# Softmax sums inverted in one narrow tile by way of DRAM, and a third key tile added on VectorE

## The chip, the cores and the metric

The kernel runs on one NeuronCore of a Trainium2 chip. The metric is device time in microseconds (us) of one execution; the kernel before took 1294.06 us (median of three runs).

## The reference

All data are float32. An attention block with normalised queries and keys is followed by a two-layer feed-forward block:

```python
# q, k, v: (8 batches, 12 heads, 448 positions, 64)
q_n, k_n = rmsnorm(q, g_q), rmsnorm(k, g_k)
scores = q_n @ k_n.T / sqrt(64)
attn = exp(scores - max)
attn = attn / (sum(attn) + 1e-9)
x = (attn @ v)           # heads side by side: 3584 tokens x 768
h = x @ w_in             # 768 x 2048
out = (h * sigmoid(h)) @ w_out   # 2048 x 768
```

## The kernel before, in words

**Couples.** The attention is done in 24 couples, numbered c = 0 to 23. A couple is four heads of one batch, and six couples (`GROUP`) make two batches. Each head has three tiles of 128 keys, `weights(c, 0)` to `weights(c, 2)`, and 64 keys left over, `left_weights(c)`. All exponentials lie in SBUF with the keys on the partitions and the 448 queries on the columns. Products with V (`weigh`) accumulate in two PSUM banks, `av0` and `av1`.

**The sums.** The softmax needs the sum of the exponentials over the keys, that is, over partitions. VectorE first adds key tile 1 into key tile 0 (`add(c, 1)`, L803). Then TensorE multiplies with a tile of ones (`sum_up`, L832): one term is four matmuls, 128 rows by 32 columns of ones, by 448 columns. For couples 0 to 4 there are three terms: key tile 2, the added tile 0, and the left-over keys. The result `t`, in a PSUM bank, holds four heads' sums, each repeated on 32 partitions.

**The inverses.** VectorE inverts `t` in two halves of 224 columns (`invert`, L841) into `sums_x`, and `spread` copies the inverses between partitions with six SBUF-to-SBUF transfers of 56 KB on the SP queue (L854 four times, and L856 twice, which wait for the former). `factors(c)` are two tiles of 128x448 in `sums_x`, taken in turn by even and odd couples. `divide(c)` (L863) multiplies the attention output of couple c with them. For couples 0 to 4 it runs late: `divide(c - 2)` stands in the visit of couple c, and `divide(3)` and `divide(4)` stand in the program after couple 4 and after couple 5. Before that VectorE has copied `av0` and `av1` out of PSUM (L1514), which frees the two banks for the next couple's `weigh`. From couple 6 on VectorE divides straight out of PSUM.

**Order.** Everything in the attention is issued by hand, engine by engine; an engine runs its instructions in the program's order and so does the SP queue, on which nearly all transfers are issued. `visit(c)` holds the scores, exponentials and products with V, `between(c)` the transposes for the next couple, the sums, and pieces of other work: `room.w_in.round()` rounds W (L126, L129, L133 on VectorE, then L137 on POOL) and loads further pieces of it (L88), and from couple 3 on TensorE is given feed-forward products (L963). Lists of closures carry work from one place to the next: for couples 0 to 2 the two closures that `sum_up` yields wait in `inverting`, of which the first runs in the middle of the next visit and the second at its end; for couples 3 and 4 they run in `between(c)`.

The order in visit(c + 1) of VectorE's work that touches this: the norm's first sum (L475), the two copies out of PSUM (L1514), the first half of the inverse, `divide`, two more norm sums, `add`, the second half of the inverse, the rounding of W.

Of the kernel before, what the change touches and what calls it, by code (L numbers as in the profile page):

```python
# [11 lines left out]
F32 = mybir.dt.float32  # L12
# [18 lines left out]
class Shapes:  # L31
    def __init__(self, q, w_in):
# [8 lines left out]
        self.HALF = self.DM // 2  # L41
        self.FULL = self.S // self.P
        self.REST = self.S - self.FULL * self.P

# [498 lines left out]
def bounded(  # L543
# [3 lines left out]
    P, D, R, J, S = z.P, z.D, z.R, z.J, z.S  # L547
    HW, HF = z.NW // 2, z.NF // 2
    mem = ctx.enter_context(tc.tile_pool(name="mem", bufs=1))
    dram = ctx.enter_context(tc.tile_pool(name="dram", bufs=1, space=bass.MemoryType.DRAM))  # L550
# [6 lines left out]
    GROUP, LATE = z.NPAIR, z.LATE  # L557
    EARLY = GROUP - 1
    SOON = 2 * GROUP - 1
    FULL = (GROUP, SOON - 1)  # L560
    LAGGED = [c for c in range(SOON - 1, NC) if c % GROUP != GROUP - 1]


    hidden = dram.tile([z.NF, P, z.B * S], F32, name="hidden")


    sets = [mem.tile([P, 2 * z.NW * S], F32, name=f"x{i}") for i in range(2)]
    sums_x = mem.tile([P, 3 * HW * S], F32, name="sums_x")
    stage = mem.tile([P, 3 * 2 * S], F32, name="stage")
    parts = mem.tile([P, 2 * S], F32, name="parts")  # L570
    work = mem.tile([P, 16 * S + z.NK], F32, name="work")
    at = 0

# [7 lines left out]
    e = [piece(4 * S).rearrange("p (i h s) -> p i h s", i=2, h=2) for _ in range(3)]  # L581
# [11 lines left out]
    n = 2 * room.COLS  # L593
# [29 lines left out]
    def factors(c):  # L623

        if c >= EARLY:
            return r
        return [sums_x[:, ts(c % 2 * 2 + i, S)] for i in range(2)]
# [9 lines left out]
    LEFT = z.KEYS  # L637
# [56 lines left out]
    n = z.NK // z.Q  # L694
# [99 lines left out]
    def add(c, j):  # L794

        def one(i):
            total = weights(c, 0)[:, i]
            if j == LEFT:
                rows = ds(i * D, D)
                total, more = total[rows], left_weights(c)[rows]  # L800
            else:
                more = weights(c, j)[:, i]
            nc.vector.tensor_tensor(out=total, in0=total, in1=more, op=ALU.add)  # L803

        return [lambda: one(0), lambda: one(1)]

    def sum_up(c):

        n = D // 2
        early = c < GROUP
        if c < GROUP:
            t = bank(S)
        elif c in LAGGED:
            t = ps_mm.tile([P, BANK], F32, name="mm")[:, 0:S]
        else:
            t = ps.tile([P, 2, BANK], F32, name="sc", bufs=2)[:, 0, 0:S]
        terms = [(0, lambda: weights(c, 0))]  # L820
        if early:
            terms = [(0, lambda: weights(c, LEFT - 1))] + terms + [(1, None)]
        if c in FULL:
            terms.insert(0, (1, None))
        if c == GROUP - 1:
            terms.insert(1, (0, lambda: weights(c, 1)))
        for k, (which, w) in enumerate(terms):
            if early and k == len(terms) - 2:
                yield
            for h in range(2):  # L830
                for i in range(2):
                    nc.tensor.matmul(  # L832
                        t[ds(h * D + i * n, n), :],
                        ones[:, which + i if which else 0],
                        left_weights(c)[:, h] if which else w()[:, i, h],
                        start=(k == 0), stop=(k == len(terms) - 1),
                    )

        def invert(half):
            rows = ts(half, S // 2)  # L840
            nc.vector.reciprocal(out=factors(c)[0][:, rows], in_=t[:, rows])  # L841

        def spread():
            mine = [a.rearrange("(h i p) s -> i h p s", h=2, i=2) for a in factors(c)]
            queues = (nc.sync, nc.gpsimd if c == GROUP - 1 else nc.sync)
            if c >= EARLY:
                nc.vector.tensor_copy(factors(c)[1], factors(c)[0])
                for i in range(2):
                    for h in range(2):
                        queues[h].dma_start(mine[i][1 - i, h], mine[i][i, h])  # L850
                return
            for h in range(2):
                for i in range(2):
                    nc.sync.dma_start(mine[1][i, h], mine[0][1, h])  # L854
            for h in range(2):
                nc.sync.dma_start(mine[0][1, h], mine[0][0, h])  # L856

        yield [lambda: invert(0), lambda: (invert(1), spread())]

    def divide(c, source):  # L860
        for i in range(2):
            x = x_of(c, i)
            nc.vector.tensor_tensor(  # L863
                out=x, in0=x if source is None else source[i], in1=factors(c)[i], op=ALU.mult
            )
# [618 lines left out]
    def visit(c):  # L1484

        beside = normalise(c + 1) if 0 < c <= GROUP else []
        if c == GROUP:
            beside = [lambda: None] + beside[2:]
        if c < NC:
            scores(c, 0, 0)  # L1490
        for step in visits.get(c, "")[:1]:
            step_of[step]()
        if lagging:
            lagging.pop(0)()
        if c == 0:
            first_q(1)
            normalise_alone(1)
            scores(c, 1, 0)
        if c == 0:
            run_all(beside[0:1])  # L1500
        else:
            weigh(c - 1, LEFT)
            weigh(c - 1, LEFT - 1, 0)
            turn(1, nc.scalar.copy if c <= GROUP else nc.vector.tensor_copy)
            run_all(beside[0:1])
            if GROUP < c < NC and c % GROUP == 0:
                sum_x(last_two(c), 0, range(2, 4))
        if c < NC:
            scores(c, 0, 1)
        if c > 0:  # L1510
            weigh(c - 1, LEFT - 1, 1)
            if c - 1 < EARLY:
                for i in range(2):
                    nc.vector.tensor_copy(x_of(c - 1, i), sums[i])  # L1514
                run_all(beside[1:2])
                if c == GROUP // 2 + 1:
                    divide(c - 2, None)
                if inverting:
                    while len(inverting) > 1:
                        inverting.pop(0)()  # L1520
                    if c > 1:
                        divide(c - 2, None)
            else:
                if lagging:
                    for i in range(2):
                        nc.vector.tensor_copy(x_of(c - 1, i), sums[i])
                    lagging.pop(0)()
                else:
                    divide(c - 1, sums)
                if c == GROUP:  # L1530
                    for i in range(1, HW):
                        sum_x(last_two(c), i, range(2))
                    for i in range(2):
                        norm.scale(c + 1, q_of(c + 1), q_of(c + 1), i, nc.vector)
                    room.w_in.round()
                run_all(beside[1:2])
                if GROUP < c < NC and c % GROUP == 0:
                    for i in range(1, HW):
                        sum_x(last_two(c), i)
                weights_in_visit(c)  # L1540
            if c + 1 < NC:
                loads["vrest"](c + 1)
        if c == NC:
            return
        if c > 0:
            scores(c, 1, 0)
        scores(c, 1, 1)
        if c <= GROUP:
            run_all(beside[2:3])
        weigh(c, 0, 1)  # L1550
        scores(c, 2, 0)
        weigh(c, 1, 1)
        turn(0, nc.scalar.copy)
        if c < GROUP:
            run_all(beside[3:4])
        scores(c, 2, 1)
        weigh(c, 0, 0)
        if c < GROUP:
            scores(c, LEFT)
        if c != GROUP - 1:  # L1560
            run_all(add(c, 1))
        weigh(c, 1, 0)
        if c < GROUP // 2:
            room.w_in.open()
        if c >= GROUP:
            scores(c, LEFT)
        if c + 1 < NC:
            loads["v"](c + 1)
        if len(inverting) == 1:
            inverting.pop()()  # L1570

    def run_all(work):
        for piece in work:
            piece()

    def between(c):
# [47 lines left out]
        late = add(c, LEFT - 1) if c >= GROUP else []  # L1624
        if c >= GROUP and c not in FULL:
            late += add(c, LEFT)
# [48 lines left out]
            while rounder.load():  # L1675
                pass

    begun, inverting, lagging = {}, [], []
    load_q(2)
    for _ in range(2):  # L1680
        room.w_in.load()
# [23 lines left out]
    for m in range(2):  # L1705
        rows = [staged() for _ in range(2)]
# [8 lines left out]
def general(  # L1715
# [130 lines left out]
    def feed_forward(b):  # L1846
        odd = b % 2
        own = mp.tile([P, z.NF, z.FULL * P], F32, name="g_own")
        if not odd:
# [72 lines left out]
```

## Time and profile before

| what | value |
|---|---|
| time of three runs | 1293.84, 1294.06, 1294.23 us |
| profiled execution, first to last instruction | 1294.6 us (0.5 us over the median of the runs) |
| TensorE busy | 1283.5 us, 99% of the span |
| VectorE busy | 971.4 us, 75% |
| ScalarE busy | 504.3 us, 39% |
| GpSimd busy | 363.5 us, 28% |
| granted TensorE clock, mean | 0.999 |
| couples 0 to 4, on TensorE | from 9 to 94 us |

The share of a busy engine is a mean over stages. The part that the change touches is the first tenth of the span, where couples 0 to 5 run with little or no feed-forward work between them, so it is read in windows of that stretch. Rows of a timeline give the start, the length, the engine, the line and the tiles of a run of like instructions, and behind that the idle time of the engine before it with what ended it. A float32 matmul stands in the records twice, so four matmuls of the program read as x8.

### The profile page before, as it was taken

To read this page: it belongs to the slowest core of one execution; us is meant where nothing else is said; L and a number is where in the kernel's file an instruction comes from. 1 tells how busy PE (TensorE), PEld (TensorE's weight loads), DVE (VectorE), ACT (ScalarE), POOL (GpSimd) and SP (SyncE) were. 2 spreads that over 40 slices of the span, in tenths; PEclk is the share of its full clock that TensorE was granted. 3 is DMA by queue.
4 is the path that set the end of the run, shared out by engine and by line. 5 is a ranking of instruction groups with operands and counts; after the bars stand their busy time and mean duration, and the time that the engine had idled before them with its cause. 6 is when DMAs were issued, how large, how long until landed. Compare 5 with 4: busy or idle time off the path is not lost.

```text
span 1294.6 us, 19931 instructions
## 1 busy us (share of the span) xinstructions
PE 1283.5 (99%) x7212; PEld 840.7 (65%) x7212; DVE 971.4 (75%) x1672; ACT 504.3 (39%) x880; POOL 363.5 (28%) x221
## 2 busy tenths in 40 slices
PE   9999999999999999999999999999999999999998
PEld 4444454444444454444544555559999999999998
DVE  6898878868666558666555886798978787878785
ACT  7967666645555554554543344310001000000000
POOL 6765454543344344343311344400000000000000
PEclk9999999999999999999999999999999999999999
DMA  9675347434444444444411466312332313141411
GB/s 232 174 193 136 104 124 197 95 83 102 112 94 91 119 91 102 108 93 93 107 50 69 149 204 219 117 66 88 100 94 86 113 67 129 51 133 48 141 39 40
DMA packets 266160, 144.15 MB, mean 111 GB/s; under 512 B 203748, under 2 KB 249956, under 8 KB 266052
## 3 DMA queue, kind: packets, MB, share of 16 engines
q1 hardware_dynamic: 265424, 141.68, 39.8%
q8 instruction: 59, 0.97, 0.3%
q0 software_dynamic: 320, 0.90, 0.2%
q14 instruction: 49, 0.40, 0.1%
q10 hardware_dynamic: 308, 0.20, 0.1%
HBM read 95.36 MB, written 41.29 MB: 106 GB/s over the span
## 4 chain that ended last, share of the span: by engine, by line
PE 97%; DVE 1%; POOL 1%; issue 0%; ACT 0%; DMA 0%; SPq 0%; ACTq 0%; DVEq 0%; POOLq 0%
PE alone L1285 23%; PE mm L963 21%; PE sc L963 11%; PE av L789 10%; PE sc L752 10%; PE mm L1285 8%; PE alone L963 7%; PE alone L1323 2%; PE mm L832 2%; PE mm L1323 1%; PE sc L643 1%; PE sc L832 1%; PE sc L674 0%; DVE work L912 0%; POOL rms L503 0%
## 5 line engine op out<-in xcount | busy, mean ns | idle before, releaser
L757 ACT ACTIVATE work<-sc,rms 128x448 f32<-128x448 f32 x318 | 182.0, 635 | 98.0 <-PE sc L752 85.7
L752 PE MATMUL sc<-work 64*64 64x448 f32 x1344 | 169.4, 543 | 1.0 <-ACT work L653 0.6
L789 PE MATMUL av<-work,rows 64*64 64x448 f32 x1272 | 155.5, 540 | 1.2 <-DVE x L1514 0.9
L963 PE MATMUL mm<-x,W 128*128 128x448 f32 x366 | 149.1, 542 | 0.0
L963 PE MATMUL mm<-sums_x,W 128*128 128x448 f32 x348 | 142.4, 542 | 0.0
L803 DVE TENSOR_TENSOR work<-work 128x896 f32<-128x896 f32 (+1 forms) x110 | 118.3, 1105 | 28.6 <-PE av L789 28.1
L530 POOL DMA_DIRECT2D out_dram<-x x2 | 1.2, 592 | 443.5 <-DVE x L912 443.5
L503 POOL TENSOR_TENSOR rms<-rms,minus_half 128x14 f32<-128x14 f32 (+4 forms) x40 | 97.4, 2437 | 86.8 <-DVE rms L499 83.3
L963 PEld LDWEIGHTS mm<-x,W 128*128 128x128 f32 x366 | 68.5, 190 | 70.3 <-issue 64.8
L1285 PE MATMUL alone<-W,rows 128*128 128x192 f32 x610 | 113.0, 326 | 0.0
L963 PEld LDWEIGHTS mm<-sums_x,W 128*128 128x128 f32 x348 | 65.1, 190 | 68.1 <-issue 62.5
L789 PEld LDWEIGHTS av<-work,rows 64*64 64x64 f32 x1272 | 65.9, 132 | 62.8 <-issue 19.3
L752 PEld LDWEIGHTS sc<-work 64*64 64x64 f32 x1344 | 60.4, 132 | 63.3 <-ACT work L757 25.3
L1285 PEld LDWEIGHTS alone<-W,rows 128*128 128x128 f32 x610 | 101.4, 190 | 0.0
L963 PE MATMUL sc<-x,W 128*128 128x448 f32 x246 | 99.6, 541 | 0.0
L984 POOL TENSOR_TENSOR stage<-parts,stage 128x448 f32<-128x448 f32 x31 | 39.8, 1285 | 169.2 <-ACT stage L983 168.9
L722 POOL TENSOR_TENSOR rms<-rms,minus_half 128x28 f32<-128x28 f32 x15 | 72.6, 4842 | 48.9 <-DVE rms L719 47.8
L963 PEld LDWEIGHTS sc<-x,W 128*128 128x128 f32 x246 | 46.4, 190 | 47.0 <-issue 46.7
L1285 PE MATMUL alone<-W,work 128*128 128x192 f32 x382 | 72.2, 326 | 0.0
L1295 ACT COPY rows<-alone 128x192 f32<-128x192 f32 x33 | 10.5, 318 | 141.5 <-PE alone L1285 136.7
L1285 PEld LDWEIGHTS alone<-W,work 128*128 128x128 f32 x382 | 63.8, 190 | 0.0
L1116 ACT ACTIVATE stage<-stage 128x896 f32<-128x896 f32 x63 | 56.8, 945 | 17.1 <-DVE stage L912 16.9
(267 smaller groups left out, 2312.8 us busy)
## 6 DMA issues: line engine op xcount, KB each, us to landing
hidden<-stage SPq DMA_DIRECT2D x63, 448.0 KB, 2.9
work<-hidden SPq DMA_DIRECT2D x21, 1024.0 KB, 5.1
rows<-in_moe_w_out_dram SPq DMA_DIRECT2D x32, 384.0 KB, 3.7
W<-in_moe_w_in_dram SPq DMA_DIRECT2D x22, 512.0 KB, 5.3
x<-hidden SPq DMA_DIRECT2D x7, 1024.0 KB, 6.1
rows<-in_q_dram SPq DMA_DIRECT2D x120, 56.0 KB, 2.2
rows<-in_k_dram SPq DMA_DIRECT2D x120, 56.0 KB, 2.3
rows<-in_k_dram SPq DMA_DIRECT2D x60, 96.0 KB, 2.6
```

The costliest lines, as they stand in the source:

```text
L503: nc.gpsimd.tensor_tensor(out=t, in0=t, in1=half, op=ALU.pow)
L722: nc.gpsimd.tensor_tensor(out=f, in0=f, in1=minus_half.to_broadcast([P, n]), op=ALU.pow)
L752: nc.tensor.matmul(two[ds(half * D, D), h, 0:S], keys[rows, ts(half, D)], qT[rows, pair, :], start=True, stop=True,)
L757: nc.scalar.activation(left_weights(c)[:, h] if j == LEFT else weights(c, j)[:, i, h], two[:, h, 0:S], AF.Exp, scale=norm.column(c, i, h, j),)
L789: nc.tensor.matmul(sums[i][ds(h * D, D), :], v, w, start=(j == 0 and step == 1), stop=(j == LEFT - 1 and step == 1),)
L803: nc.vector.tensor_tensor(out=total, in0=total, in1=more, op=ALU.add)
L832: nc.tensor.matmul(t[ds(h * D + i * n, n), :], ones[:, which + i if which else 0], left_weights(c)[:, h] if which else w()[:, i, h], start ...
L963: nc.tensor.matmul(t, self.left(name, s), self.right(name, s), start=s == ends[0], stop=s == ends[1])
L984: nc.gpsimd.tensor_tensor(out=done[1, 2], in0=u2, in1=p5, op=ALU.add)
L1116: nc.scalar.activation(t, t, AF.Silu)
L1285: nc.tensor.matmul(t, x[:, i], y, start=i == ORDER[0], stop=i == ORDER[-1])
L1323: nc.tensor.matmul(o, a[:, 2 * i + m, t], right_one(name, i)[:, m], start=n == 0, stop=n == len(steps) - 1,)
```

## The change

For couples 0 to 4 the inverses take another way. `gather` copies `t` from PSUM to SBUF, and a transfer lays one row for each head (four rows of 448) out as 128 partitions by 14 columns in a new tile `spot`. `invert_all` inverts `spot`, stores it in a DRAM tile `totals` (four rows of 448, one such tile for even and one for odd couples), and a last transfer reads it back into `sums_x`: the first two rows side by side (896 numbers) on partitions 0 to 63, the last two on 64 to 127. For couples 0 to 2 the two closures stand where the halves of the inverse stood; for couples 3 and 4 `gather` stands in `between(c)` and `invert_all` in the visit of the next couple. From couple 5 on nothing changes.

For couples 0 to 2 VectorE also adds key tile 2 into tile 0, and the product with ones has two terms, first the left-over keys, then the added tile.

```diff
+    LIGHT = GROUP // 2
+    totals = [dram.tile([4, S], F32, name=f"totals{i}") for i in range(2)]
+    spot = mem.tile([P, 4 * S // P], F32, name="spot")
...
         terms = [(0, lambda: weights(c, 0))]
-        if early:
+        if c < LIGHT:
+            terms = [(1, None)] + terms
+        elif early:
             terms = [(0, lambda: weights(c, LEFT - 1))] + terms + [(1, None)]
...
-            if early and k == len(terms) - 2:
+            if early and k == max(1, len(terms) - 2):
                 yield
...
-            for h in range(2):
-                for i in range(2):
-                    nc.sync.dma_start(mine[1][i, h], mine[0][1, h])
-            for h in range(2):
-                nc.sync.dma_start(mine[0][1, h], mine[0][0, h])
-        yield [lambda: invert(0), lambda: (invert(1), spread())]
+        def gather():
+            t_sums = factors(c)[0]
+            nc.vector.tensor_copy(t_sums, t)
+            rows = t_sums.rearrange("(n p) s -> n p s", n=4)[:, 0]
+            nc.sync.dma_start(spot, rows.rearrange("n (p e) -> n p e", p=P // 4))
+        def invert_all():
+            d = totals[c % 2]
+            nc.vector.reciprocal(out=spot, in_=spot)
+            nc.sync.dma_start(d.rearrange("n (p e) -> (n p) e", p=P // 4), spot)
+            source = d.rearrange("(h one i) s -> h one (i s)", one=1, i=2)
+            nc.sync.dma_start(sums_x[:, ts(c % 2, 2 * S)], source.to_broadcast([2, D, 2 * S]))
+        if c < LIGHT:
+            yield [gather, invert_all]
+        elif c < EARLY:
+            spreading.append(invert_all)
+            yield [gather]
+        else:
+            yield [lambda: invert(0), lambda: (invert(1), spread())]
...  visit(c)
+                if spreading:
+                    spreading.pop()()
...
+        if c < LIGHT:
+            run_all(add(c, LEFT - 1))
```

In the kernel with the change the lines stand a little further down: L803 is L806, L832 is L837, L863 is L880, and the new lines are L858 and L860 (`gather`) and L864, L865 and L867 (`invert_all`).

VectorE in the visit of couple 2 and behind it, where couple 0 is divided and couple 1 inverted, before (`x` is the attention output or, in L475, the squares; `mm` is the bank of the sums):

```order
L841 RECIPROCAL sums_x<-mm 128x224
L863 TENSOR_TENSOR x_172<-x_172,sums_x 128x448 x2
L475 TENSOR_REDUCE rms_61<-rows 128x8
L475 TENSOR_REDUCE rms_61<-x_173 128x6
L499 TENSOR_SCALAR rms_61<-rms_61 128x14
L803 TENSOR_TENSOR work<-work 128x896 x2
L841 RECIPROCAL sums_x<-mm 128x224
L126 TENSOR_SCALAR W<-W 128x512
```

and now:

```order
L858 COPY sums_x<-mm 128x448
L880 TENSOR_TENSOR x_174<-x_174,sums_x 128x448 x2
L475 TENSOR_REDUCE rms_61<-rows 128x8
L475 TENSOR_REDUCE rms_61<-x_175 128x6
L499 TENSOR_SCALAR rms_61<-rms_61 128x14
L806 TENSOR_TENSOR work<-work 128x896 x4
L864 RECIPROCAL spot<-spot 128x14
L126 TENSOR_SCALAR W<-W 128x512
```

Each half of the inverse has become one short instruction, the adds are four instead of two, and the order around them is as it was.

The SP queue from the visit of couple 1 on, where couple 0's sums are handled (`rows` are inputs of q, k and v), before:

```order
L273 DMA x_173<-in_q_dram 112x4x256
L331 DMA rows<-in_v_dram 128x4x64
L334 DMA rows<-in_v_dram 64x2x64 x2
L318 DMA rows<-in_v_dram 128x4x128
L854 DMA sums_x<-sums_x 32x448 x4
L856 DMA sums_x<-sums_x 32x448 x2
L294 DMA rows<-in_k_dram 128x6x64
```

and now:

```order
L273 DMA x_175<-in_q_dram 112x4x256
L860 DMA spot<-sums_x 128x1x14
L331 DMA rows<-in_v_dram 128x4x64
L334 DMA rows<-in_v_dram 64x2x64 x2
L318 DMA rows<-in_v_dram 128x4x128
L865 DMA totals_172<-spot 128x14
L867 DMA sums_x<-totals_172 128x1x896
L294 DMA rows<-in_k_dram 128x6x64
```

The six short copies are gone, a transfer of 7 KB has come in ahead of the loads of V, and a store of 7 KB and a read of 448 KB ahead of those of K.

More of the change, by code (lines that the diff above doesn't have):

```diff
@@ L845, in spread @@
             queues = (nc.sync, nc.gpsimd if c == GROUP - 1 else nc.sync)
-            if c >= EARLY:
-                nc.vector.tensor_copy(factors(c)[1], factors(c)[0])
-                for i in range(2):
-                    for h in range(2):
-                        queues[h].dma_start(mine[i][1 - i, h], mine[i][i, h])
-                return
-            for h in range(2):
-                for i in range(2):
-                    nc.sync.dma_start(mine[1][i, h], mine[0][1, h])
-            for h in range(2):
-                nc.sync.dma_start(mine[0][1, h], mine[0][0, h])
-        yield [lambda: invert(0), lambda: (invert(1), spread())]
+            nc.vector.tensor_copy(factors(c)[1], factors(c)[0])
+            for i in range(2):
+                for h in range(2):
+                    queues[h].dma_start(mine[i][1 - i, h], mine[i][i, h])
+        def gather():
[16 more added lines that the diff above has]
+            yield [lambda: invert(0), lambda: (invert(1), spread())]
     def divide(c, source):
@@ L1676, in between @@
                 pass
-    begun, inverting, lagging = {}, [], []
+    begun, inverting, spreading, lagging = {}, [], [], []
     load_q(2)
```

## The prediction

> **What bounds the kernel now.** I read the page's busy shares and its chain of waits first, then windows of the stretch where the change sits, then the timeline of VectorE at the divisions, since these consume what the change makes.
>
> ```profile
> PE 1283.5 (99%) x7212; PEld 840.7 (65%) x7212; DVE 971.4 (75%) x1672; ACT 504.3 (39%) x880; POOL 363.5 (28%) x221
> PE 97%; DVE 1%; POOL 1%; issue 0%; ACT 0%; DMA 0%; SPq 0%; ACTq 0%; DVEq 0%; POOLq 0%
> ```
>
> TensorE works 1283.5 of 1294.6 us and the chain runs along it. Little can be won but TensorE's own work; much can be lost if it is made to wait. The next rows are windows: length, then busy time of PE, PEld, DVE, ACT and POOL, the granted clock, the DMA share and GB/s.
>
> ```profile
> 30.00:60.00 30.00, 29.91 (x298) 12.59 (x294) 25.95 (x39) 27.27 (x52) 21.99 (x14) 1.00 0.75 206
> 60.00:90.00 30.00, 28.58 (x242) 13.13 (x246) 27.62 (x38) 22.76 (x43) 21.79 (x13) 1.00 0.63 165
> 104.94:116.91 11.97, 11.97 (x109) 5.31 (x105) 11.62 (x17) 8.38 (x15) 6.91 (x6) 1.00 0.30 73
> ```
>
> In this stretch VectorE, 75% busy over the span, is at 87%, 92% and 97%. It runs in order, so what stops it there is made up slowly. These are its five divisions by the factors in question, `divide(0)` to `divide(4)`, then the first direct division of couple 6 and TensorE's weight load behind it:
>
> ```profile
> 46.57 1.09 DVE L863 TENSOR_TENSOR x<-x,sums_x 128x448 f32<-128x448 f32 x2
> 63.31 1.97 DVE L863 TENSOR_TENSOR x<-x,sums_x 128x448 f32<-128x448 f32 x2 [1.28 <-DMA sums_x<-sums_x]
> 80.37 2.01 DVE L863 TENSOR_TENSOR x<-x,sums_x 128x448 f32<-128x448 f32 x2
> 91.27 1.15 DVE L863 TENSOR_TENSOR x<-x,sums_x 128x448 f32<-128x448 f32 x2
> 104.94 1.81 DVE L863 TENSOR_TENSOR x<-x,sums_x 128x448 f32<-128x448 f32 x2 [0.19 <-DMA sums_x<-sums_x]
> 116.91 1.16 DVE L863 TENSOR_TENSOR x<-av,work 128x448 f32<-128x448 f32 x2
> ```
>
> ```profile
> 117.89 0.52 PEld L789 LDWEIGHTS av<-work,rows 64*64 64x64 f32 x8 [0.23 <-issue]
> ```
>
> Two of the five already wait for the last copy of the spread. The row at 116.91 reads `av` out of PSUM, and TensorE's next product into `av` starts at 117.89 behind it: there, late factors become late TensorE.
>
> **The change part by part.** Prices, by groups of the first 135 us (busy time, mean ns of one):
>
> ```profile
> L841 DVE RECIPROCAL sums_x<-mm 128x224 f32<-128x224 f32 x10 | 15.3, 1543 | 0.0
> L1514 DVE COPY x<-av 128x448 f32<-128x448 f32 x10 | 5.7, 617 | 0.0
> L499 DVE TENSOR_SCALAR rms<-rms 128x14 f32<-128x14 f32 x7 | 1.7, 238 | 0.2
> L803 DVE TENSOR_TENSOR work<-work 128x896 f32<-128x896 f32 x10 | 11.3, 1173 | 0.0
> ```
>
> *VectorE.* Per couple, two inverses (3.09 us) go; a copy of 128x448 (0.62, by L1514) and an inverse of 128x14 come. The latter has no row: it lies between a 128x14 operation of another kind (0.24) and the old inverse (1.54); cost per column is what the inverse's rows show (1.54 for 224), and I take 0.2. VectorE gains 2.3 us in each of five couples. Two more adds cost couples 0 to 2 about 2.1 us each (row at 33.65, below). So its work shrinks by 11.4 - 6.3 = 5 us; its order is kept, so its waits decide.
>
> *TensorE.* One term of the sums goes from couples 0 to 2:
>
> ```profile
> 36.66 0.96 PE L832 MATMUL mm<-work,ones 128*32 128x448 f32 x8
> 37.44 0.94 PE L832 MATMUL mm<-x,ones 128*32 128x448 f32 x8
> 38.19 0.94 PE L832 MATMUL mm<-work,ones 128*32 128x448 f32 x8
> 33.65 2.10 DVE L803 TENSOR_TENSOR x<-x,work 128x896 f32<-128x896 f32 x2
> ```
>
> From start to start a term takes 0.76, so 2.3 us in all. But the added tile now needs four adds: they start at 33.65 and end at 37.8 (2.05 later than before), while its term would start at 37.44, so about 0.4 is waited in each couple. Net -1.1, between -2.3 (adds early) and 0.
>
> *The transfers.* Six copies of 56 KB become three steps, each waiting for the one before: spot, the 7 KB store, and the 448 KB read.
>
> ```profile
> 33.58 0.33 SPq L273 DMA_DIRECT2D x<-in_q_dram  x1
> 40.67 2.80 SPq L856 DMA_DIRECT2D sums_x<-sums_x  x2
> x<-in_q_dram SPq DMA_DIRECT2D x1, 448.0 KB, 5.1
> DMA to landing us min/median/max: 1.9/2.7/7.8
> ```
>
> Spot is queued right behind a q load, which for couple 0 takes 5.1 us from 33.9; so spot lands at 38.9, 1.1 after the adds end. VectorE, which formerly had its data in PSUM, now waits for a transfer ahead of each inverse; behind it are queued the rounding of W, the next norm sums and the copies out of `av`, and on SP, behind the store and the read that wait for the inverse, the K and W loads. The store, at 7 KB, gets the smallest landing of the tile's copies, 1.9, and 0.2 to start: 2.1.
>
> The read has no counterpart. It takes two source rows, each 64 times: 128 pieces of 3584 bytes. Its price hangs on how many DMA engines carry it. Nearest from the side of large ones, a plain 448 KB transfer between DRAM and SBUF, whose two sides have 128 rows:
>
> ```profile
> stage<-ahead SPq DMA_DIRECT2D x1, 448.0 KB, 3.6
> ```
>
> And from the side of few rows, the two loads of the gains, one row each; they alone are on queue 10 of the first 115 us. Last come the packets while the two L856 copies, 32 rows each, run, and a saturated window.
>
> ```profile
> q10 hardware_dynamic: 4, 0.00, 0.0%
> W<-in_g_q_dram ACTq DMA_DIRECT2D x1, 0.2 KB
> W<-in_g_k_dram ACTq DMA_DIRECT2D x1, 0.2 KB
> DMA packets 75, 0.09 MB, mean 35 GB/s; under 512 B 32, under 2 KB 74, under 8 KB 74
> 32.00:34.00 2.00, 2.00 (x21) 0.67 (x20) 1.10 (x4) 2.00 (x5) 1.65 (x3) 1.00 1.04 408
> ```
>
> Each copy left 16 packets under 512 bytes: one end mark for each engine. The gain loads left four packets in two transfers, so one of data and one mark each: one engine. The count of engines thus follows the rows that a transfer steps through. 408 GB/s at a share of 1.04 is 24.5 GB/s an engine. 458,752 bytes then take 1.2 us on 16, 9.4 on two, 18.7 on one; with 1.9 to land, 3.1, 11.3 and 20.6. The ends are 3.1 and 20.6. I take two engines, 11.3, since the outermost step of the source counts two rows and the nearest case, a count of one, got one engine.
>
> [...]
>
> *The sum.* Couple 0: spot 38.9, inverse 0.2, store 2.1, read 11.3: 52.5, where `divide(0)` stood at 46.57. VectorE stands there, and the next inverse is behind it: one turn of a loop. The norm sums between take 1.4 by these starts:
>
> ```profile
> 47.58 0.68 DVE L475 TENSOR_REDUCE rms<-rows 128x8 f32<-128x512 f32 x1
> 48.96 2.10 DVE L803 TENSOR_TENSOR work<-work 128x896 f32<-128x896 f32 x2
> ```
>
> Couple 1: division 1.1, norm sums 1.5, four adds 4.1, about 1 for spot (two of its engines are still draining), then 13.6 (0.2, 2.1, 11.3): 73.8 against 63.31. Couple 2, two adds fewer and spot in time: 1.1 + 1.5 + 2.1 + 13.6 = 18.3, so 92.1 against 80.37. Couple 3's inverse stands right behind `divide(2)`, without adds, but its spot stands behind loads on the two engines: about 1.9 MB are under way, a sixteenth of it each, an estimated 5.4 with landing; with 13.6 that is 19.0: 111.1 against 91.27. Couple 4 likewise, 19.5 with the longer division row: 130.6 against 104.94. The factors are 25.7 late. From there VectorE is busy 11.62 of 11.97 us, so 0.3 is regained up to 116.91, and TensorE at 117.89 starts its product 25.4 late. TensorE's net gain of 1.1 lies ahead of that wait and is swallowed. TensorE then is the bound again and cannot make it up. Against the profiled execution 1294.6 + 25.5 = 1320.1; that execution stands 0.5 over the median of the runs, so 1319.6, rounded to 1320. This case's own range is 1306 (half of each wait hidden) to 1338 (the K loads, queued behind the read, add 3 us to each turn).
>
> **The rivals.** *First: 16 engines carry the read, no change.* It lands in 3.1 to 3.6, and only spot makes VectorE late.
>
> ```profile
> 60.36 0.98 PE L789 MATMUL av<-x,rows 64*64 64x448 f32 x8 [0.45 <-DVE rms L475]
> 79.19 1.13 PE L789 MATMUL av<-work,rows 64*64 64x448 f32 x6 [0.94 <-DVE x L1514]
> 74.89 2.96 DVE L841 RECIPROCAL sums_x<-mm 128x224 f32<-128x224 f32 x2
> ```
>
> The wait at 60.36 grows by some 1.5 through VectorE's spot waits; the one at 79.19 (0.94) goes, as the pair of inverses ahead of that copy out of PSUM becomes a 0.62 copy; `divide(4)`, which already waits, gets 1 later; the products bring -1.1. 1294.1 + 1.5 - 0.9 + 1.0 - 1.1 = 1294.6, about 1295. For it: all large transfers here run on 16, and the destination does have 128 partitions. Against it: the one-row loads.
>
> *Second, not slower: faster, by hidden transfers.* If spot lands before the adds end (37.8 for couple 0) and the read in under 4 us, VectorE never waits. Then the products bring -1.1, the wait at 79.19 -0.94, that at 60.36 -0.45, and that of 104.94 -0.19: 1291.4. Against it: the q load's 5.1 us, which holds spot until 38.9.
>
> *Third: the read runs on some number between.* On four engines it takes 4.7 + 1.9 = 6.6, each turn is 4.7 shorter, and the five turns leave few microseconds: 1298 to 1306. Nothing in the trace speaks for it but that two ends are known.
>
> **How the numbers follow.** Two engines 0.74, the first rival 0.18, the second 0.04, the third 0.04. About 0.2%, 2.6 us, is what a measurement of this kernel can tell from no change. The forecast and the third rival are slower; of the first, 0.14 is within 2.6 us, 0.02 each beyond. That gives faster 0.06, same 0.14, slower 0.80. The range 1292 to 1338 takes in most of the first rival and leaves out the second and the forecast's upper tail.
>
> **What the changed profile would show.** Right: the reads from `totals` land some 11 us after issue, and the DMA busy share is low while they run; VectorE's divisions wait for DMA with `sums_x<-totals`, and start near 52, 74, 92, 111 and 130; TensorE has idle stretches adding up to some 25 us between 50 and 145, ended by copies or divisions on VectorE; behind that, all rows are those of before, shifted. The term of the sums behind four adds shows a wait of about 0.4. Wrong: reads that land in under 4 us (the first two rivals); an inverse of 128x14 near 1 us; or a granted clock under 1.00 behind the long idle stretches, which would put time on top that the sum lacks.

## The result and the profile after

The changed kernel takes 1327.91 us (median of five runs, 1324.57 to 1330.07) against 1294.10: a ratio of 1.0255, 95% interval 1.0244 to 1.0265, slower by 33.8 us. The forecast was 1320, range 1292 to 1338.

First the page of the changed kernel, then its windows (columns as before).

```profile
PE 1293.8 (98%) x7188; PEld 846.5 (64%) x7188; DVE 965.5 (73%) x1678; ACT 504.1 (38%) x880; POOL 360.8 (27%) x221
PE 92%; DMA 4%; DVE 2%; ACT 1%; SPq 0%; issue 0%; ACTq 0%; DVEq 0%
sums_x<-totals SPq DMA_DIRECT2D x5, 448.0 KB
```

```profile
30.00:60.00 30.00, 25.96 (x230) 11.04 (x226) 21.01 (x35) 23.04 (x43) 18.43 (x12) 0.94 0.67 202
60.00:90.00 30.00, 27.28 (x231) 11.07 (x229) 19.36 (x35) 19.81 (x39) 16.97 (x11) 0.95 0.35 102
129.50:144.85 15.35, 10.57 (x89) 4.62 (x81) 10.82 (x18) 6.79 (x13) 3.14 (x3) 1.00 0.21 56
```

DMA has come into the chain of waits, with 4%. TensorE does fewer matmuls and is nevertheless busy 10 us longer, and the granted clock, 1.00 in all three windows before, is 0.94 and 0.95 in the first two. VectorE, 87%, 92% and 97% busy in the three windows before, is now at 70%, 65% and 70%: it stands idle more of the time. Its timeline tells where: these are the five late divisions, now L880, and the first direct one.

```profile
51.57 1.16 DVE L880 TENSOR_TENSOR x<-x,sums_x 128x448 f32<-128x448 f32 x2 [5.41 <-DMA sums_x<-totals]
74.39 1.16 DVE L880 TENSOR_TENSOR x<-x,sums_x 128x448 f32<-128x448 f32 x2 [6.30 <-DMA sums_x<-totals]
93.52 1.16 DVE L880 TENSOR_TENSOR x<-x,sums_x 128x448 f32<-128x448 f32 x2 [4.31 <-DMA sums_x<-totals]
112.87 1.16 DVE L880 TENSOR_TENSOR x<-x,sums_x 128x448 f32<-128x448 f32 x2 [6.05 <-DMA sums_x<-totals]
133.86 1.16 DVE L880 TENSOR_TENSOR x<-x,sums_x 128x448 f32<-128x448 f32 x2 [8.13 <-DMA sums_x<-totals]
144.85 1.16 DVE L880 TENSOR_TENSOR x<-av,work 128x448 f32<-128x448 f32 x2
```

All five wait for the read, 30.2 us together. The reads themselves stand in the DMA rows. The issue of couple 0's read comes first, then the DMA share (in tenths) and the rate from 40.3 to 52 us, in 40 slices of 0.29 us.

```profile
40.31 0.56 SPq L867 DMA_DIRECT2D sums_x<-totals  x1
```

```profile
DMA  0000100399611111111311431114215795311965
GB/s 0 0 0 0 25 25 37 104 236 275 177 53 49 49 49 49 49 61 49 105 49 49 110 86 74 49 54 121 70 58 144 184 227 151 109 59 32 191 106 160
```

Between 43.8 and 45.9 us the rate is 49 GB/s in six slices of seven, at a share of 0.12 (two of 16): two engines at 24.5 GB/s and fourteen empty. The trace has the read as 128 packets of 3584 bytes, 0.144 us each in the median, and they run from 41.64 to 51.06, two at a time on average. From the issue at 40.31 to the division at 51.57 are 11.3 us; for the others, by their issues (62.91, 81.91, 101.33, 122.67), 11.2 to 11.6.

TensorE's waits in the stretch from 50 to 146 us that are over 1 us, all behind VectorE, none behind a DMA:

```profile
57.06 2.72 PE L837 MATMUL mm<-work,ones 128*32 128x448 f32 x8 [4.04 <-DVE work L806]
77.86 1.59 PE L837 MATMUL mm<-x,ones 128*32 128x448 f32 x5 [2.64 <-DVE x L806]
102.10 1.59 PE L837 MATMUL mm<-work,ones 128*32 128x448 f32 x5 [3.00 <-DVE work L806]
118.97 2.29 PE L792 MATMUL av<-x,rows 64*64 64x448 f32 x8 [5.62 <-DVE x L1531]
145.53 2.29 PE L792 MATMUL av<-work,rows 64*64 64x448 f32 x8 [5.46 <-DVE x L880]
```

The last is the product into `av` that the prediction puts at 117.89. That is the row of its weight load, which is 27.6 us later now. The matmuls themselves stood here before:

```profile
118.26 0.93 PE L789 MATMUL av<-work,rows 64*64 64x448 f32 x8
```

They are 27.3 us later. Over the next 5 us of work the distance grows, and from the matmuls that stood at 123 us before on to the last one, all stand 30.0 to 30.3 us later than in the first profile.

### The profile page after: what moved, and what is told of

It is laid out like the page before. It is cut to its first block, busy times and chain, and to the rows that moved or that the text cites. A ratio compares the mean times of both kernels' runs of the same rounds, so it can differ in the third digit from the quotient of the medians.

```text
span 1324.7 us, 19869 instructions
## 1 busy us (share of the span) xinstructions
PE 1293.8 (98%) x7188; PEld 846.5 (64%) x7188; DVE 965.5 (73%) x1678; ACT 504.1 (38%) x880; POOL 360.8 (27%) x221
## 4 chain that ended last, share of the span: by engine, by line
PE 92%; DMA 4%; DVE 2%; ACT 1%; SPq 0%; issue 0%; ACTq 0%; DVEq 0%
PE alone L1302 22%; PE mm L980 20%; PE sc L980 11%; PE av L792 9%; PE sc L755 9%; PE mm L1302 8%; PE alone L980 7%; DMA sums_x<-totals 3%; PE alone L1340 2%; PE mm L837 1%; DMA spot<-sums_x 1%; PE mm L1340 1%; PE sc L837 1%; DMA totals<-spot 0%; DVE work L929 0%; DVE x L880 0%
## 5 line engine op out<-in xcount | busy, mean ns | idle before, releaser
L755 PE MATMUL sc<-work 64*64 64x448 f32 x1344 | 175.6, 554 | 1.0 <-ACT work L656 0.7
L792 PE MATMUL av<-work,rows 64*64 64x448 f32 x1272 | 160.3, 549 | 5.7 <-DVE x L880 5.5
L806 DVE TENSOR_TENSOR work<-work 128x896 f32<-128x896 f32 (+1 forms) x114 | 121.5, 1096 | 28.9 <-PE av L792 28.4
L755 PEld LDWEIGHTS sc<-work 64*64 64x64 f32 x1344 | 63.9, 135 | 63.4 <-ACT work L760 24.2
L980 PEld LDWEIGHTS sc<-x,W 128*128 128x128 f32 x246 | 46.4, 190 | 47.1 <-issue 46.5
```

The costliest lines, as they stand in the source:

```text
L755: nc.tensor.matmul(two[ds(half * D, D), h, 0:S], keys[rows, ts(half, D)], qT[rows, pair, :], start=True, stop=True,)
L792: nc.tensor.matmul(sums[i][ds(h * D, D), :], v, w, start=(j == 0 and step == 1), stop=(j == LEFT - 1 and step == 1),)
L980: nc.tensor.matmul(t, self.left(name, s), self.right(name, s), start=s == ends[0], stop=s == ends[1])
```

## The experiments

**The kernel before, once more.**

> The kernel before, unchanged, profiled once more. The profiled execution shown for it took 1296.4 us, 2 us over the median of its runs. Expected: a span near 1292.5 us; where its rows stand earlier than those of the profile shown tells which 2 us of that profile were its own. All theories expect the same here.

It took 1294.29 us, with a span of 1292.5. From 14 to 57 us its matmuls agree with those of the first profile within 0.06 us, and from 80 us on they stand 1.9 us earlier on average. So the waits of 0.45 and 0.94 us at 60.36 and 79.19 of that first profile, on which two rivals of the prediction counted, belonged to that execution: here no wait of TensorE behind VectorE is listed between 14 and 170 us.

**The read in two.** Instead of one read with two source rows, one for each half:

```diff
-            nc.sync.dma_start(sums_x[:, ts(c % 2, 2 * S)], source.to_broadcast([2, D, 2 * S]))
+            for h in range(2):
+                out = sums_x[ds(h * D, D), ts(c % 2, 2 * S)]
+                nc.sync.dma_start(out, source[h].to_broadcast([D, 2 * S]))
```

> The changed kernel, with the 448 KB read issued as two reads of 224 KB, one for each half of the partitions; each now steps through 64 rows on both sides (the one stored row, 64 times with stride zero, into 64 partitions). Nothing else differs. Theory A (the read is slow because its outermost step counts two, so that two DMA engines carry it): each read runs on 16 engines, lands within 3 to 4.5 us of its issue, the DMA rate while it runs is far above the 49 GB/s of the changed kernel, the five divisions start within 2 us of those of the kernel before (46.6, 63.3, 80.4, 91.3, 104.9), and the time is 1293 to 1298 us; I take 1295. Rival B (the three-step chain is the culprit: spot behind the q load, the inverse on VectorE behind spot, the store, whatever carries the read): the read lands sooner, but at least a third of the loss stays, 1305 us or more. Rival C (repeating one DRAM row 64 times is itself slow, at any number of engines): reads still land 8 us or more after issue, 1315 us or more.

It took 1299.03 us, ratio 1.0032 (1.0021 to 1.0044): 28.9 of the 33.8 us are gone. The rows are a window from the middle of couple 0's reads, the median landing of the ten, and couple 4's division:

```profile
42.30:45.50 3.20, 2.69 (x30) 0.75 (x24) 3.17 (x6) 3.20 (x7) 2.43 (x2) 1.00 0.98 219
sums_x<-totals SPq DMA_DIRECT2D x10, 224.0 KB, 4.0
108.69 1.16 DVE L882 TENSOR_TENSOR x<-x,sums_x 128x448 f32<-128x448 f32 x2 [4.07 <-DMA sums_x<-totals]
```

The DMA share is 0.98 instead of 0.12. Rivals B and C fall. But 4.6 us over the kernel before stay, four over theory A's figure and one over its range: `divide(4)` still waits 4.07 us, since its store and read together take 8 us behind the inverse. TensorE waits 2.06 us behind that division and 1.4 us, in two waits, behind copies out of PSUM.

**62 and 2 rows instead of 64.** The same two reads, each cut once more:

```diff
+                for first, n in ((0, 62), (62, 2)):
+                    out = sums_x[ds(h * D + first, n), ts(c % 2, 2 * S)]
+                    nc.sync.dma_start(out, source[h].to_broadcast([n, 2 * S]))
```

> As the run with two reads (64 partitions each), but each of the two is cut into one of 62 partitions and one of 2: the same source row, the same bytes, the same targets, two issues more. Theory A (the number of engines follows the number of rows stepped through; 62 has no divisor up to 16 but 2 and 1): two engines carry all of it, 49 GB/s while they run, reads land 10 us or more after issue, and the loss is back: 1315 to 1335 us. Rival (what was slow was one transfer with a source of two rows, or the broadcast as a single transfer): 1297 to 1302 us, as with 64.

It took 1332.88 us, ratio 1.0297 (1.0279 to 1.0314): the whole loss is back, and 5 us more. These are the DMA rows from 43 to 50 us and couple 0's division:

```profile
DMA  2214345589930111110211262111144111136899
GB/s 76 85 60 114 94 116 117 145 198 218 240 98 29 61 61 41 41 41 20 82 41 41 76 173 78 42 61 61 47 133 123 66 41 61 41 105 184 219 278 266
52.14 1.16 DVE L883 TENSOR_TENSOR x<-x,sums_x 128x448 f32<-128x448 f32 x2 [6.26 <-DMA sums_x<-totals]
```

Bytes, source and targets are those of the run before; 64 has become 62 and 2, with two more issues for each couple. Between these two runs it is the number of rows that decides (a DMA share of 0.98 with 64 above, digits of 0 to 2 from 45.1 to 46.8 us here), neither the broadcast nor the single transfer.

**The same read with nobody waiting.** The kernel before, with this behind the spread of couples 0 to 3:

```diff
+            if c < EARLY - 1:
+                source = own["q"][0, 0].rearrange("(n one a) d -> n one (a d)", one=1, a=14)[0:2]
+                nc.sync.dma_start(
+                    sums_x[:, ts(2 + c % 2, 2 * S)], source.to_broadcast([2, D, 2 * S])
+                )
```

> The kernel before, with one read more for each of couples 0 to 3, in the old way of inverting: behind the last copy of the spread, two rows of 896 numbers of q are read 64 times each into a part of sums_x that nothing uses until couple 5. So the two engines are occupied 9.4 us four times, and loads behind it share them, but no instruction waits for the read. Theory A1 (the loss of the change is the wait of the divisions for their data): the loads behind land some 9 us later but most are not needed that soon; 1294 to 1300 us. Rival D (the loss is the queue: K, W, q and V loads behind the read on its two engines stop ScalarE and VectorE by themselves): 1306 us or more. In between: both.

It took 1323.28 us, ratio 1.0224 (1.0207 to 1.0241). My theory A1 fell: four reads that nothing waits for cost 29 us. The rows are TensorE's waits of over 1 us, and the division that waits longest, for the last short copy of the old spread:

```profile
65.84 1.77 PE L789 MATMUL av<-x,rows 64*64 64x448 f32 x8 [5.95 <-DMA rows<-in_v_dram]
120.34 1.77 PE L789 MATMUL av<-x,rows 64*64 64x448 f32 x8 [14.09 <-DMA rows<-in_v_dram]
108.32 1.16 DVE L868 TENSOR_TENSOR x<-x,sums_x 128x448 f32<-128x448 f32 x2 [11.79 <-DMA sums_x<-sums_x]
```

So V is late by the backlog (the transfers that queue up behind the read) alone, and so are the old spread's copies, for which the divisions wait 23.3 us in all. That a later transfer has a part on the two engines shows in the changed kernel's trace. The K load behind couple 0's read (128x6x64, so 768 rows of 256 bytes) was issued at 40.97, and in the window from 41.6 to 44 us the packets are these:

```profile
DMA packets 716, 0.28 MB, mean 117 GB/s; under 512 B 686, under 2 KB 686, under 8 KB 716
```

Of the 686 short ones, 672 are rows, which is fourteen sixteenths of 768, and 14 are end marks, packets of 4 bytes. No further row of that size runs before 46.5 us, and what is left over of this load and of those behind it runs only from about 51 us on, as the read ends.

**The same bytes on 16 engines.** The unused read in two of 64 rows, as above.

> The kernel before with the four unused reads of the earlier run, the same bytes from the same rows of q, but each as two reads of 64 rows. Theory A: 16 engines carry each, 1.2 us instead of 9.4, and loads behind it are in time: 1294 to 1297 us. Rival (448 KB more traffic at that place, or one DRAM row read 64 times, is what hurt): 1310 us or more, as with the single read (1323).

It took 1299.45 us, ratio 1.0034 (1.0021 to 1.0048): 24 of the 29 us go. The range of theory A is missed by 2.5 us, though: the 1.8 MB added to a busy stretch cost 5 us on 16 engines too (a DMA share of 0.81 at 190 GB/s from 44 to 47 us; TensorE waits 1.22 us for V at 61.10).

**The read off SP's queue.** The changed kernel, its read issued with `nc.gpsimd.dma_start`.

> The changed kernel with its 448 KB read of two rows issued by GpSimd instead of SP, nothing else: it no longer stands in SP's queue ahead of the K, W, q and V loads. Theory A2 (either of two consequences of a two-engine read is enough by itself: the divisions wait for its data, and loads behind it on its engines come late): the divisions still wait 4 to 8 us for the read, 1310 to 1330 us. Rival D (the loss is the blocked queue alone): loads are in time, and 1296 to 1304 us.

It took 1338.33 us, ratio 1.0332 (1.0314 to 1.0349), 8 us over what A2 expected. Rival D falls: the read's place in SP's order is not what makes it costly.

```profile
sums_x<-totals POOLq DMA_DIRECT2D x5, 448.0 KB, 13.8
58.59 1.16 DVE L880 TENSOR_TENSOR x<-x,sums_x 128x448 f32<-128x448 f32 x2 [11.96 <-DMA sums_x<-totals]
```

The K and W loads now stand ahead of the read and beside it, so it lands later, and couple 0's division waits 12.0 us instead of 5.4. The read has its two source rows here as before, so this run does not part the two consequences of a slow read, the backlog and the divisions' wait for its data. What is shown is that the backlog of four idle reads costs 29 us by itself, and that the changed kernel, with five reads and the divisions waiting for them, loses 33.8: the two do not simply add up. What the wait for the data would cost without the backlog stays open.

**The adds alone.** The kernel before, with two more adds and a term less for couples 0 to 2.

> The kernel before with the second part of the change alone: for couples 0 to 2 VectorE adds the third key tile and the sums have two terms; inverses and spread are the old ones. VectorE gets 6.3 us more with nothing taken off it, TensorE 2.3 us less. Theory: each couple's last term waits some 0.4 us for the adds, VectorE, at 87 to 92% there, is late by up to 2 us at the next copies out of PSUM, and the gain is about eaten: 1293 to 1297 us, I take 1295. Rival: the adds are a main cause of the loss (waits of 4.0, 2.6 and 3.0 us at the last term of the sums in the changed kernel): 1303 us or more.

It took 1296.74 us, ratio 1.0017 (1.0007 to 1.0026): slower by 2.3 us, at the upper end of what was expected. TensorE waits 0.97 us twice, at 45.43 and 61.91, behind VectorE's copies out of PSUM; the kernel before has no such wait in its second profile.

**The new way of inverting alone, read in two.** Three terms everywhere.

> As the run with two reads, but without the adds: three terms of the sums on TensorE for all five couples, so only the way of inverting differs from the kernel before. Theory A: VectorE is relieved of 2.3 us in each of five couples and pays for the waits on spot (about 1 us each, up to 4 for couple 3); the waits at 60.36, 79.19 and 104.94 of the kernel before (0.45, 0.94, 0.19) shrink: 1292.5 to 1296 us, I take 1293.5. If the adds were free beside it, this run is 1 to 2 us slower than the one with two reads; if they are what keeps VectorE late, it is faster. Rival B (the chain of steps): 1303 us or more.

It took 1298.12 us, ratio 1.0029 (1.0020 to 1.0039), 2 us over the range: the waits that I expected to shrink are not there in the second profile of before, and `divide(4)` waits 3.05 us here. The run with the adds is 0.9 us slower than this one, which is less than the spread of either's runs; no gain of the adds shows here either.

**Couple 4 in the old way, spot ahead of the q load.**

```diff
+                if len(inverting) > 1:
+                    inverting.pop(0)()
                 run_all(beside[1:2])
...
-        elif c < EARLY:
+        elif c < EARLY - 1:
             spreading.append(invert_all)
```

> A candidate: two reads of 64 partitions, couple 4 inverted and spread in the old way, and for couples 0 to 2 the copy and spot stand ahead of the next q load instead of behind it; the adds as in the change. In the run with two reads TensorE waited 2.06 us at couple 6 behind divide(4), which waited 4.07 us for the read, and VectorE waited 0.76 and 1.10 us for spot. Theory: the wait at couple 6 goes, those for spot go, what stays are the waits behind the four adds (0.5 and 0.85 us at the copies out of PSUM): 1294 to 1297 us, I take 1296. If it is not under 1297.5, the rest of the loss of that run comes from elsewhere.

It took 1295.00 us, ratio 1.0002 (0.9992 to 1.0012). The loss is gone; how much each of the two edits brought, this run does not tell. What the adds cost and bring is read from TensorE's rows of couple 1, first in the second profile of the kernel before, then in this run:

```profile
36.62 0.96 PE L832 MATMUL mm<-work,ones 128*32 128x448 f32 x8
37.40 0.93 PE L832 MATMUL mm<-x,ones 128*32 128x448 f32 x8
38.15 0.94 PE L832 MATMUL mm<-work,ones 128*32 128x448 f32 x8
39.01 0.98 PE L752 MATMUL sc<-work 64*64 64x448 f32 x8
```

```profile
36.72 0.96 PE L837 MATMUL mm<-work,ones 128*32 128x448 f32 x8
37.49 1.62 PE L837 MATMUL mm<-x,ones 128*32 128x448 f32 x8
39.04 0.98 PE L755 MATMUL sc<-work 64*64 64x448 f32 x8
```

A term is gone and the other one takes 1.62 us instead of 0.93, as it waits for the adds inside the group; the next scores start where they did.

**The last term later.** For couples 0 to 2 it now follows the next couple's first scores and the products of the left-over keys.

```diff
             weigh(c - 1, LEFT)
+            if waiting:
+                inverting.extend(next(waiting.pop()))
             weigh(c - 1, LEFT - 1, 0)
```

> The candidate before (two reads, couple 4 in the old way, spot ahead of the q load), and for couples 0 to 2 the last term of the sums, which waits for the four adds, is put later on TensorE: behind the next couple's first scores and the products of the left-over keys, some 2.2 us of work. In the candidate this term starts 0.4 to 2.0 us later than in the kernel before, so that the 0.75 us saved in each couple were waited away. Theory: the waits go, the 2.3 us of TensorE's work are won for the most part: 1292 to 1293.8 us, I take 1292.6. Rival (VectorE, with two more adds, is late anyway at the next copies out of PSUM, wherever the term stands): 1294.5 to 1296 us.

It took 1296.05 us, ratio 1.0009 (1.0000 to 1.0018): the theory is missed, and the run is 1 us slower than without the move.

```profile
38.93 0.98 PE L755 MATMUL sc<-work 64*64 64x448 f32 x8 [0.85 <-ACT work L679]
37.85 1.02 ACT L679 ACTIVATE work<-sc,gains 128x896 f32<-128x896 f32 x1
```

The wait for the adds is gone and another has come out from under it: the scores need the transposed keys, which ScalarE writes until 38.87. Against the kernel before, two terms, 1.5 us, have left the place ahead of the scores, and in each of the three couples the scores come only some 0.6 us earlier against the work before them; the rest is this wait of 0.82 to 0.86 us. So of the 0.75 us of one term at most 0.6 was to be won, and the wait for the adds, 0.7 us in couple 1 of the run before, is longer. The late term then takes 1.0 us where it now stands, and behind it the products are 0.45, 0.9 and 1.35 us later than in the kernel before, couple by couple.

**The same order with the old inverses.** Adds and late term in the kernel before.

> The kernel before with the adds and the late last term, but with the old inverses and spread for all couples. VectorE has 6.3 us more to do in couples 0 to 2 and nothing taken off it. Theory: VectorE is late at the copies out of PSUM of couples 1 and 2, as in the run with the adds alone (TensorE waited 0.97 us there twice): 1294.5 to 1297 us. Rival (the adds cost only through the place of the last term, and the narrow inverse is not needed): 1292 to 1293.8 us.

It took 1296.85 us, ratio 1.0014 (1.0005 to 1.0023): 0.8 us over the run with the narrow inverse. Together with the next run this says that the load which the narrow inverse takes off VectorE is worth something only where the adds have put it on.

**The narrow inverse alone, all mended.** Couples 0 to 3, reads of 64 rows, spot early, no adds.

> The candidate with couple 4 in the old way, two reads of 64 partitions and spot ahead of the q load, without the adds: three terms of the sums in all couples. [...] In the second profile of the kernel before, TensorE has no wait of 0.2 us or more behind VectorE between 14 and 170 us, so taking 2.3 us a couple off VectorE has nothing to shorten. Theory: 1294.0 to 1295.0 us, the kernel before within 0.05%. Rival (VectorE's load there costs TensorE something that the waits do not show): 1293.5 us or less.

It took 1294.39 us, ratio 0.9995 (0.9986 to 1.0004), the same as the kernel before. In each of the four couples a copy of 0.62 us and an inverse of 0.24 stand for two halves of 1.54, and TensorE, which did not wait for VectorE, gains nothing. No version tried beats the kernel before.

## Why the prediction was right, and where it was not

- **The read on two engines**: right, and it is the cause: the read runs for 9.4 us at 49 GB/s, and 11.2 to 11.6 pass from issue to use (11.3 forecast). With 64 rows 28.9 of the 33.8 us are gone, with 62 and 2 all are back. By marks, shares and rates the runs show one engine for one row (the marks of the gain loads), 16 for 32 rows (the marks of each copy), two for two (49 GB/s at a DMA share of 0.12), two for 62 and 2 (48 GB/s on average from 45.3 to 46.8 us, two of 24.5) and 16 for 64 (a share of 0.98).
- **The loop**: the divisions were forecast at 52.5, 73.8, 92.1, 111.1 and 130.6 and stood at 51.57, 74.39, 93.52, 112.87 and 133.86. The wait for spot cost VectorE 1.51, 0, 4.92 and 0.69 us from couple 1 on; about 1, 0, 5.4 and 5.4 were forecast. That spot shares engines with the read, which these terms take, no run shows; the waits are what was measured. The last turn is 1.5 us longer than reckoned all the same: couple 4's inverse, at 120.94, stands behind 6.1 us of VectorE's other work (113.95 to 120.07), which the step had left out.
- **What the loop stands for** was told too narrowly. The sum has the divisions wait for the read's data. That is what the changed kernel shows, but the run with idle reads loses 29 us though nothing waits for the reads: there TensorE waits 20.0 us for V, and 0.6 us behind a division. The backlog on the two engines alone costs nearly as much, by another way.
- **The sum**: 25.5 was forecast (its own steps, 25.7 less 0.3, give 25.4), and 33.8 came. The product into `av` came 27.3 us late, which is 1.9 more. From there the clock took 3.0 more, the item named as not in the sum: after that wait the granted clock was 0.50 for 6.28 us (below). And the base was misjudged: the table of the profile before compares a span with the runs' times, but a run's time is its span and 1.8 to 1.9 us around it. That execution took 1296.4 us, 2.3 over the median and not 0.5. The 1.9 us by which its product was later than in the second profile lay ahead of the last waits and were swallowed by them, so 1.9 more belong to the difference. The profiled run of the changed kernel is 1.3 us under its median. Together, 25.4 + 1.9 + 3.0 + 1.9 + 1.3 is 33.5.
- **The range**: 3 us in each of five turns are 15, so its upper end should have been 1335 and not 1338; the measured time lies under both.
- **The signs**: TensorE's idle stretches add up to 21 us and not some 25. Three of the five long ones, 9.7 us, are ended by the adds of couples 2, 3 and 4, to which VectorE comes late, and not by copies or divisions. The wait of 0.4 us at the term behind four adds is there in couples 0 and 1, where that term takes 1.43 and 1.46 us instead of 0.93; in couple 2 it has become 4.04. The clock under 1.00, named as a sign of being wrong, did appear (0.50 behind three of the waits).
- **TensorE's net gain of 1.1 us** was wrong in sign. The adds alone cost 2.3 us. The step took the start-to-start time of a term for what its removal saves: in couple 1 the next scores start where they did, held by the adds and, right behind them, by ScalarE's copy of the transposed keys. And it put at nothing that the adds make VectorE late at its copies out of PSUM, where TensorE waits 1.9 us in the run with the adds alone.
- **The inverse of 128x14** took 0.24 us (0.2 was taken), the copy 0.62 (0.62 was taken).
- **The first rival**, 16 engines, priced at 1295: the run was 1299.0. It counted on two waits that belonged to that one execution, on the products' gain, and on `divide(4)` 1 us later, where it waits 4.07.

## What to carry to other kernels

Before a transfer is priced by its bytes, count the rows it steps through on both sides: in these runs couple 0's factors, 448 KB, were 11.3 us from issue to use with 2 rows and 11.9 with 62, while the halves of 64 rows landed in 4.0 in the median. On two engines the read also held up the transfers behind it that had a part there, and not only its own reader: four reads that nothing waited for cost 29 us. An instruction removed from the busiest engine gained only what the next one there did not have to wait for anyway, here at most 0.6 us of a term's 0.75. And small waits in one profile are worth checking against a second, or at least against the median of the runs.

## What the hardware showed beside

These are windows of the changed kernel right behind TensorE's waits; the granted clock is the third column from the end, and the last row is the whole stretch at half clock behind the last wait:

```profile
57.06:61.00 3.94, 3.94 (x16) 0.93 (x20) 2.36 (x5) 0.00 (x0) 0.37 (x1) 0.50 0.96 174
77.86:79.50 1.64, 1.56 (x10) 0.42 (x13) 1.60 (x4) 0.00 (x0) 1.64 (x1) 1.00 0.66 181
102.10:104.00 1.90, 1.82 (x13) 0.52 (x16) 1.83 (x4) 0.00 (x0) 1.90 (x1) 1.00 0.36 92
118.97:122.00 3.03, 3.03 (x16) 1.91 (x20) 2.03 (x5) 0.07 (x1) 1.67 (x1) 0.50 0.32 115
145.50:149.00 3.50, 3.47 (x18) 2.16 (x22) 3.43 (x7) 1.78 (x4) 2.42 (x1) 0.50 0.98 257
145.53:151.81 6.28, 6.28 (x34) 3.94 (x38) 6.14 (x12) 3.08 (x7) 2.93 (x2) 0.50 0.92 248
```

After waits of 4.04, 5.62 and 5.46 us it is exactly half, after 2.64 and 3.00 us it is full. Behind the first two stretches at half clock TensorE waits for VectorE again (2.64 us at 77.86, 5.46 at 145.53), and what they cost can have gone into those waits; how much, no run shows. Behind the last stretch no such wait is listed up to 180 us: 6.28 us at half clock are 3.1 us of lost work, and the matmuls are 3.0 us later than the wait alone makes them.
